# A new order for the first four tiles of a fused convolution and feed-forward kernel, and a doubling moved into an evacuation

## The chip, the cores and the metric

The kernel runs on one core of one Trainium2 chip. The metric is the time of one execution on the device in microseconds (us). Five timed runs of the kernel before gave a median of 720.44 us, from 720.09 to 720.65.

## The reference

```python
# attention part: a causal 7-tap convolution, one softmaxed filter for each of 8 heads
w = softmax(weight, axis=-1)                       # [8, 7]
x_pad = zeros of 6 rows before x                   # x is [8, 4096, 192]
out[b, s, h, g] = sum_k w[h, k] * x_pad[b, s + k, h, g]
# feed-forward part, on the 32768 rows of out
h = out @ w_in                                     # [32768, 192] @ [192, 2048]
g = h * cos(h)
result = g @ w_out                                 # [32768, 2048] @ [2048, 192]
```

Input and output are float32; the kernel computes with bfloat16 operands and float32 sums.

## The kernel before, in words

**Tiles and units.** The 32768 rows are cut into 64 tiles of 512 rows (`t`) and 32 units of 1024 rows (`u`), two tiles to a unit. For a unit the following happens. SP loads it (`load_unit`, L75, 768 KB) and the 16 rows at its block edges (`load_edges`, L69). POOL casts it to bfloat16 (`cast_unit`, L179). TensorE convolves it with banded matrices (`conv_part` through `conv_mm`, L190), in two halves of the channels called `c = 0` and `c = 1`. ACT copies each half out of PSUM into the tile `ct` (`conv_out`, L205, one copy a bank). `ct` holds each row of 64 channels twice, because the matmuls that follow run two at a time on the two halves of TensorE's rows; POOL writes the second copy (`double_unit`, L247). SP transposes `ct` into `cT` with a DMA (`turn_unit`, L253). POOL mends the first six rows of each block from the edge rows (`mend_edges`, L259).

**The feed-forward of a tile.** Eight chunks `h0` to `h7`, each six matmuls (`mm1`, L347) into one of three PSUM buffers named `h`. For each chunk ACT computes the cosine (`cs`, L354) and DVE multiplies (`g`, L358; the step is called `s0` to `s7`). The product with w_out is cut into steps (`mm2_step`, L377), 64 a tile. A step issues a matmul on the lower rows for one phase and one on the upper rows for the phase before, so that the first 32 steps of all have one matmul and the others two. The outputs gather in two PSUM banks, `o_ps0` and `o_ps1`, which ACT copies out (`evac`, L389) and SP stores (`store`, L392). Where one bank changes from the lower rows to the upper ones, and between the two parts of a split convolution, a no-operation on SP's queue (`Turn`, L164) passes the order from one matmul to the next: SP's queue carries loads, transposes, stores and these turns, in program order.

**The order is written by hand.** A string for each tile gives TensorE's order: `h3` is a chunk, `m7` seven steps, `c1` and `c2` the two parts of a conv half, `p` and `q` marks at which an output half is complete and at which DMA issues and POOL work are put. A second string gives ACT's (and with it DVE's): `s3` a cosine and a product, `ec1` and `ec2` the evacuations of a conv half, `P` and `Q` those of an output half. An entry of ACT's string is put out as soon as what it needs stands in the program. Tiles 0 and 1 have strings of their own, because there units 1 and 2 are convolved whole (the halves `d` and `c`), the other tiles use `PE_ORDER` and `ACT_ORDER`. In tile 0 a conv half uses the banks `o_ps0` and `o_ps1` (`o_banks`), from tile 1 on an `h` buffer (`ring_banks`).

**The start.** The first half of unit 0 (512 rows, which is tile 0) is convolved and transposed on TensorE (`conv_first`, `turn_first`). Its second half comes at the entry `r` in tile 0: `conv_rest`, then POOL's doubling, then the transpose by DMA, then the loads of unit 2, then POOL's two casts of w_out (L445). The loads of unit 3 and the doubling of unit 1 follow at the end of tile 0; the transpose of unit 1, the cast of unit 3 and the mending of unit 1 at `q` of tile 1.

Of the kernel before, what the change touches and what calls it, by code (L numbers as in the profile page):

```python
# [16 lines left out]
def kernel(  # L17
# [12 lines left out]
    G = D // H  # L30
# [3 lines left out]
    NB = T // 128  # L34
    U = 1024
    NU = NTOK // U
    UB = U // 128
# [149 lines left out]
    def conv_mm(u, c, ps, i, rows, n0, n1, prev=0, **flags):  # L187

        h = 4 * c + i
        return nc.tensor.matmul(  # L190
            out=ps[i // 2][:, 0 : (n1 - n0) * 2 * G].rearrange("p (n k i r) -> p i n k r", n=n1 - n0, k=NC, i=2)[:, i % 2],
            lhsT=band[rows, h, 128 if prev else 0 : 256 if prev else 128],
            rhs=bf[u][rows, n0:n1, h * G : (h + 1) * G].rearrange("p n (k r) -> p n k r", k=NC),
            skip_group_check=True, **flags)

    def conv_out(u, c, ps, n0, m0, m1, copy, double=False, banks=(0, 1)):

        for b in banks:
            w0 = (2 * c + b) * 2 * R
            o = ct_tiles[u][:, m0:m1, :, :, w0 : w0 + 2 * R].rearrange("p n k t w -> p (n k) t w")  # L200
            i = ps[b][:, (m0 - n0) * 2 * G : (m1 - n0) * 2 * G].rearrange("p (m t w) -> p m t w", t=1, w=2 * R)
            if double:
                copy(o, i.to_broadcast([128, (m1 - m0) * NC, 2, 2 * R]))
            else:
                copy(o[:, :, 0, :], i[:, :, 0, :])  # L205
# [5 lines left out]
    def o_banks():  # L211
        return [o_pools[b].tile([128, T], FP32, name="o_ps%d" % b) for b in range(2)]

    def conv_part(u, c, banks, whole=False):


        ps = banks()
        sides = [slice(0, 64), slice(64, 128)]

        def mm(i, rows, **flags):  # L220
            return conv_mm(u, c, ps, i, sides[rows], 0, UB + 1, **{"start": False, "stop": False, **flags})

        if whole:
            for i in range(4):
                conv_mm(u, c, ps, i, slice(0, 128), 0, UB + 1, start=i % 2 == 0, stop=i % 2 == 1)
            yield
        else:
            mm(0, 0, start=True)
            mm(2, 1, start=True)
            turn = Turn()  # L230
            turn.mark(mm(1, 0), mm(3, 1))
            yield
            turn.wait(mm(2, 0), mm(0, 1))
            mm(3, 0, stop=True)
            mm(1, 1, stop=True)
        yield
        if c == 0 and u not in ct_tiles:
            ct_tiles[u] = ct_pool.tile([128, UB + 1, NC, 2, 64], BF16, name="ct")
        for b in range(2):
            conv_out(u, c, ps, 0, 0, UB + 1, nc.scalar.copy, banks=(b,))  # L240
            yield
# [3 lines left out]
    def double_unit(u, n0=0, n1=UB + 1):  # L245
        ct = ct_tiles[u]
        nc.gpsimd.tensor_copy(out=ct[:, n0:n1, :, 1, :], in_=ct[:, n0:n1, :, 0, :])  # L247
# [29 lines left out]
    for i, k in enumerate("DPDPDPADPDPADPAD"):  # L277
        q, rows = divmod(i, 4)
# [5 lines left out]
    copies = [nc.scalar.copy, nc.vector.tensor_copy]  # L284
# [33 lines left out]
    def conv_rest():  # L318
        banks = o_banks()
        for c in range(2):  # L320
            for i in range(4):
                for prev in range(2):
                    conv_mm(0, c, [b[:, 4 * G * 2 * c :] for b in banks], i, slice(0, 128), NB + 1 - prev, UB + 1 - prev, prev,
                            start=c == 0 and prev == 0 and i % 2 == 0, stop=c == 1 and prev == 1 and i % 2 == 1)
        for b in range(2):
            for c in range(2):
                conv_out(0, c, [x[:, 4 * G * 2 * c :] for x in banks], NB, NB, UB, copies[1 - b], banks=(b,))

    conv_first()
    turn_first(0)  # L330
# [20 lines left out]
    def gcu(t, j, h, n0=0, n1=NB):  # L351
        cs = cos_pool.tile([128, 2, T], BF16, name="cs")
        part = slice(n0 * 128, n1 * 128)
        nc.scalar.activation(out=cs[:, :, part], in_=h[:, :, part], func=AF.Sin, bias=math.pi / 2.0, scale=1.0)  # L354
        if j == 0 and n0 == 0:
            g_tiles[t] = gpool.tile([128, NF, T], BF16, name="g")
            g_tiles.pop(t - 3, None)
        nc.vector.tensor_tensor(out=g_tiles[t][:, 2 * j : 2 * j + 2, part], in0=h[:, :, part], in1=cs[:, :, part], op=ALU.mult)  # L358
# [27 lines left out]
    def evac(t, b):  # L386
        if b == 0:
            o_sb[t] = opool.tile([128, NB, D], FP32, name="o_sb")
        nc.scalar.copy(o_sb[t][:, 2 * b : 2 * b + 2, :].rearrange("p s d -> p (s d)"), o_ps.pop((t, b))[:, 0 : 2 * D])  # L389

    def store(t, b0=0, b1=2):
# [8 lines left out]
    PE_ORDER = "h0 m7 c1 m6 c2 m4 h1 m7 q h2 h3 m12 h4 m10 h5 m10 h6 h7 p m8"  # L400
    ACT_ORDER = "s0 ec1 ec2 s1 Q s2 s3 s4 s5 P s6 s7"

    PE_FIRST = ["h0a h0b h1 r h2 h3 h4 d1 d2 h5 h6 c1 c2 h7 p m12",
                "h0 m8 h1 m12 q h2 h3 h4 m4 d1 d2 m8 h5 m8 h6 c1 c2 m8 h7 m4 p m8"]
    ACT_FIRST = ["s0a s0b s1 s2 s3 s4 ed1 ed2 s5 s6 ec1 ec2 s7", "s0 s1 s2 s3 s4 ed1 ed2 s5 s6 ec1 ec2 P s7"]

    HALVES = {"": (0, NB), "a": (0, NB // 2), "b": (NB // 2, NB)}
    step = 0
    for t in range(NT + 2):
        u, second = divmod(t, TPU)  # L410
        cu, cc = (u + TPU, second) if t >= TPU else (1 + t, 1)
        conv = {"c": conv_part(cu, cc, ring_banks if t else o_banks, t < TPU) if cu < NU else iter(())}
        if t < TPU:
            conv["d"] = conv_part(cu, 0, ring_banks if t else o_banks, True)
        act, done, h = (ACT_ORDER if t > 1 else ACT_FIRST[t]).split(), set(), {}

        def flush():
            while act:
                k = act[0]
                need = {"P": "p", "Q": "q", "e": k[1:2] + "2"}.get(k[0], "h" + k[1:])  # L420
                if need not in done:
                    return
                act.pop(0)
                if k == "P" and 0 <= t - 1 < NT:
                    evac(t - 1, 0)
                elif k == "Q" and 0 <= t - 2 < NT:
                    evac(t - 2, 1)
                elif k[0] == "e":
                    next(conv[k[1]], None)
                elif k[0] == "s" and t < NT:  # L430
                    gcu(t, int(k[1]), h.pop(k[1:]), *HALVES[k[2:]])

        for k in (PE_ORDER if t > 1 else PE_FIRST[t]).split():
            if k[0] == "h" and t < NT:
                h[k[1:]] = mm1(t, int(k[1]), *HALVES[k[2:]])
            elif k[0] in conv:
                next(conv[k[0]], None)
            elif k == "r":
                conv_rest()
                double_unit(0, NB, UB)  # L440
                turn_unit(0, NB, UB)
                load_unit(2)
                load_edges(2)
                for q in range(2):
                    nc.gpsimd.tensor_copy(out=wo[:, q * HP : (q + 1) * HP], in_=wo_f[:, q * HP : (q + 1) * HP])  # L445
            elif k[0] == "m":
                for q in range(step, step + int(k[1:])):
                    mm2_step(q)
                step += int(k[1:])
            elif k[0] == "p":  # L450
                assert step % (2 * STEPS) == 0
            elif k[0] == "q":
                assert step % (2 * STEPS) == STEPS
            done.add(k)
            flush()

            if k == "q":
                if second == 0 and t and u + 1 < NU:
                    turn_unit(u + 1)
                    mend_edges(u + 1)  # L460
                if t == 1:
                    turn_unit(1)
                    cast_unit(3)
                    mend_edges(1)
                if second == 0 and u + 3 < NU:
                    cast_unit(u + 3)
                if second == 1 and t > 1 and cu < NU:
                    double_unit(cu)
                if t == NT + 1:
                    store(NT - 1, 1, 2)  # L470
            if k == "p":
                if t < NT + 1 and 0 <= t - 2:
                    store(t - 2)
                if t == NT:
                    store(NT - 1, 0, 1)
                if second == 1 and u + 4 < NU:
                    load_unit(u + 4)
                    load_edges(u + 4)
        if t == 0:
            double_unit(1)  # L480
            load_unit(3)
            load_edges(3)
            cast_unit(2)
        if t == 1:
            double_unit(2)
# [30 lines left out]
```

## Time and profile before

| what | value |
|---|---|
| median of five timed runs | 720.44 us |
| the profiled execution, its own time | 720.38 us |
| its span | 718.7 us |
| TensorE matmul busy | 708.2 us, 99% |
| ACT busy | 617.8 us, 86% |
| DVE busy | 611.3 us, 85% |
| POOL busy | 149.8 us, 21% |
| granted TensorE clock, mean | 0.999 |

The profile is of one execution; its times count from the start of its span. "PE" is TensorE's matmuls and "PEld" its weight loads. A line such as "L377" is the line of the kernel before. In square brackets stands how long an engine was idle before an instruction, and what it waited for. Matmuls are pipelined: the length of a row of matmuls holds the depth of the last one, so that rows overlap by some 0.2 us.

### The profile page before, as it was taken

The numbers are of one execution on the slowest core, as the hardware profiler recorded it, in microseconds if no ns is written. First come the engines' busy times: TensorE is split into PE (matmuls) and PEld (weight loads), VectorE is DVE, ScalarE is ACT, GpSimd is POOL, SyncE is SP. The second block draws the span as 40 slices with busy tenths as digits, with TensorE's granted clock in tenths as the row PEclk, the third lists the DMA queues.
The fourth block names the chain that finished last, engine by engine and source line by source line (L and its number), as shares of the span: only waits on it lengthen the run. The fifth ranks groups of instructions, "written<-read, shape, count | busy, mean of one in ns | idle before, by whom it ended". The sixth has DMA issues, their size and how long they took to land.

```text
span 718.7 us, 26316 instructions
## 1 busy us (share of the span) xinstructions
PE 708.2 (99%) x11827; PEld 529.8 (74%) x11827; DVE 611.3 (85%) x536; ACT 617.8 (86%) x781; POOL 149.8 (21%) x124
## 2 busy tenths in 40 slices
PE   7899999999999999999999999999999999999997
PEld 3577777777777777777777777777777777777776
DVE  6788888888888888888888888888888888888984
ACT  7888888888888898888888888888888888888884
POOL 5621112221122221022220222220222221121000
PEclk9999999999999999999999999999999999999999
DMA  8745544455534356534455434566434555424312
GB/s 216 182 122 144 137 93 130 85 135 145 126 108 116 87 144 145 113 108 113 102 145 145 117 101 104 114 144 145 109 109 95 124 145 143 103 67 89 80 46 67
DMA packets 183664, 85.24 MB, mean 119 GB/s; under 512 B 111616, under 2 KB 183168, under 8 KB 183552
## 3 DMA queue, kind: packets, MB, share of 16 engines
q1 hardware_dynamic: 183128, 82.78, 47.0%
q8 instruction: 92, 1.51, 0.9%
q0 software_dynamic: 416, 0.79, 0.7%
q14 instruction: 20, 0.16, 0.1%
q10 hardware_dynamic: 8, 0.00, 0.0%
HBM read 31.36 MB, written 25.17 MB: 79 GB/s over the span
## 4 chain that ended last, share of the span: by engine, by line
PE 95%; DMA 2%; POOL 1%; DVE 1%; ACT 0%; issue 0%; SPq 0%; DVEq 0%; POOLq 0%
PE o_ps L377 46%; PE h L347 45%; PE h L190 3%; DMA wo_f<-in_moe_w_out_dram 1%; DMA x_f<-in_x_dram 1%; PE h L377 0%; POOL x_bf L179 0%; POOL wo L445 0%; PE o_ps L292 0%; DVE g L358 0%; DVE band L279 0%; DVEq L511 0%; ACT cs L354 0%; POOL mask L128 0%; DVE ct L298 0%
## 5 line engine op out<-in xcount | busy, mean ns | idle before, releaser
L358 DVE TENSOR_TENSOR g<-h,cs 128x1024 bf16<-128x1024 f32 (+1 forms) x513 | 603.4, 1217 | 94.0 <-ACT cs L354 89.2
L354 ACT ACTIVATE cs<-h 128x1024 bf16<-128x1024 f32 (+1 forms) x513 | 511.5, 1026 | 59.1 <-PE h L347 52.0
L377 PE MATMUL o_ps<-wo,g 64*128 64x192 bf16 x8128 | 423.8, 243 | 1.7 <-ACT o_sb L389 0.6
L377 PEld LDWEIGHTS <-g 64*128 64x128 bf16 x8192 | 362.0, 94 | 86.1 <-SPq L164 1.2
L347 PE MATMUL h<-cT,w 64*128 64x512 bf16 (+1 forms) x3078 | 398.2, 376 | 0.3 <-DVE cT L316 0.2
L347 PEld LDWEIGHTS <-w 64*128 64x128 bf16 x3078 | 154.3, 94 | 85.6 <-issue 1.1
L259 POOL COPY cT<-cT 128x144 bf16<-128x144 bf16 x31 | 9.6, 310 | 496.8 <-DMA cT<-ct 393.3
L179 POOL CAST x_bf<-x_f 128x1728 bf16<-128x1728 f32 (+1 forms) x32 | 80.6, 2518 | 8.7 <-DMA x_f<-in_x_dram 8.6
L205 ACT CAST ct<-h 128x432 bf16<-128x432 f32 x120 | 56.4, 522 | 27.4 <-PE h L190 26.9
L389 ACT COPY o_sb<-o_ps 128x384 f32<-128x384 f32 x127 | 60.0, 473 | 4.9 <-PE o_ps L377 4.9
L247 POOL COPY ct<-ct 128x1728 bf16<-128x1728 bf16 (+1 forms) x32 | 51.3, 1604 | 17.6 <-ACT ct L205 17.0
L190 PE MATMUL h<-x_bf,band 64*128 64x216 bf16 (+1 forms) x472 | 42.7, 254 | 0.9 <-POOL x_bf L179 0.9
L190 PEld LDWEIGHTS <-band 64*128 64x128 bf16 (+1 forms) x496 | 22.2, 94 | 7.1 <-issue 4.5
L105 PE MATMUL o_ps<-zero 128*128 128x512 bf16 x12 | 5.5, 630 | 1.3 <-DVE zero L100 1.3
L377 PE MATMUL h<-wo,g 64*128 64x192 bf16 x64 | 5.8, 243 | 0.0
L190 PE MATMUL o_ps<-x_bf,band 128*128 128x96 bf16 (+1 forms) x24 | 1.9, 222 | 2.5 <-POOL x_bf L179 2.5
L105 PEld LDWEIGHTS <-zero 128*128 128x128 bf16 x15 | 1.7, 129 | 3.5 <-issue 2.2
L205 ACT CAST ct<-o_ps 128x432 bf16<-128x432 f32 (+1 forms) x6 | 2.4, 460 | 1.1 <-PE o_ps L190 1.1
L445 POOL CAST wo<-wo_f 128x1536 bf16<-128x1536 f32 x2 | 2.9, 1470 | 1.0 <-DMA wo_f<-in_moe_w_out_dram 1.0
L389 ACT COPY o_sb<-h 128x384 f32<-128x384 f32 x1 | 0.5, 479 | 2.4 <-PE h L377 2.4
L115 ACT ACT_TABLE_LOAD x1 | 1.3, 1283 | 1.4 <-PEq L500 1.4
L292 PEld LDWEIGHTS <-band 128*128 128x128 bf16 x32 | 1.1, 102 | 1.1 <-POOL band L279 1.0
(47 smaller groups left out, 27.7 us busy)
## 6 DMA issues: line engine op xcount, KB each, us to landing
out_dram<-o_sb SPq DMA_DIRECT2D x63, 384.0 KB
x_f<-in_x_dram SPq DMA_DIRECT2D x31, 768.0 KB
x_f<-in_x_dram SPq DMA_DIRECT2D x31, 96.0 KB
wo_f<-in_moe_w_out_dram SPq DMA_DIRECT2D x4, 384.0 KB
x_f<-in_x_dram SPq DMA_DIRECT2D x2, 384.0 KB
w<-in_moe_w_in_dram POOLq DMA_DIRECT2D x2, 384.0 KB, 6.2
cT<-ct SPq DMA_TRANSPOSE x32
out_dram<-o_sb SPq DMA_DIRECT2D x2, 192.0 KB
```

Of the source, the lines that this page charges most:

```text
L105: nc.tensor.matmul(out=bank, lhsT=zero[:, 0:128], rhs=zero, start=True, stop=True)
L179: copy(out=bf[u][:, n0 + o : n1 + o, :].rearrange("p n (h k r) -> p (n h) k r", k=NC, r=R), in_=x_tiles[u][:, n0:n1, :].rearrange("p n (h ...
L190: return nc.tensor.matmul(out=ps[i // 2][:, 0 : (n1 - n0) * 2 * G].rearrange("p (n k i r) -> p i n k r", n=n1 - n0, k=NC, i=2)[:, i % 2], ...
L205: copy(o[:, :, 0, :], i[:, :, 0, :])
L247: nc.gpsimd.tensor_copy(out=ct[:, n0:n1, :, 1, :], in_=ct[:, n0:n1, :, 0, :])
L259: nc.gpsimd.tensor_copy(out=cT[u][:, 0:UB, :, 0 : K - 1], in_=cT[u][:, UB].rearrange("p c (n t) -> p n c t", t=16)[:, :, :, 8 : 8 + K - 1])
L347: nc.tensor.matmul(out=h[:, i, n0 * 128 : n1 * 128], lhsT=w[rows, k, j, :], rhs=c[rows, m0 + n0 : m0 + n1, k, :], start=(k == 0), stop=(k ...
L354: nc.scalar.activation(out=cs[:, :, part], in_=h[:, :, part], func=AF.Sin, bias=math.pi / 2.0, scale=1.0)
L358: nc.vector.tensor_tensor(out=g_tiles[t][:, 2 * j : 2 * j + 2, part], in0=h[:, :, part], in1=cs[:, :, part], op=ALU.mult)
L377: m = nc.tensor.matmul(out=o_ps[tt, b][:, si * D : (si + 1) * D], lhsT=g_tiles[tt][rows, f, s * 128 : (s + 1) * 128], rhs=wo[rows, f // 2, ...
L389: nc.scalar.copy(o_sb[t][:, 2 * b : 2 * b + 2, :].rearrange("p s d -> p (s d)"), o_ps.pop((t, b))[:, 0 : 2 * D])
L445: nc.gpsimd.tensor_copy(out=wo[:, q * HP : (q + 1) * HP], in_=wo_f[:, q * HP : (q + 1) * HP])
```

## The change

The doubling of the second half of unit 0 is no longer a POOL copy after the evacuation; the evacuation itself writes both copies, on DVE and ACT, as `conv_first` does. The transpose of that half then follows `conv_rest` directly, still behind the four loads of w_out and ahead of the loads of unit 2 in SP's queue. Tiles 0 to 3 get new strings. In tile 0, `h2` stands before `r` and `h5` before the conv halves, and the 12 steps at its end go to tile 1; tile 1 begins with 8 steps and ends with `h7`; tiles 2 and 3 have strings of their own, of which tile 2's begins with 9 steps, the first conv part and 1 step before `h0`. At the end of tile 3 as many steps have been put out as before (200), and from tile 4 on the strings are the same. The number of instructions differs on POOL alone, which has one less.

```diff
         for b in range(2):
             for c in range(2):
-                conv_out(0, c, [x[:, 4 * G * 2 * c :] for x in banks], NB, NB, UB, copies[1 - b], banks=(b,))
+                conv_out(0, c, [x[:, 4 * G * 2 * c :] for x in banks], NB, NB, UB, copies[1 - b], True, (b,))
...
-    PE_FIRST = ["h0a h0b h1 r h2 h3 h4 d1 d2 h5 h6 c1 c2 h7 p m12",
-                "h0 m8 h1 m12 q h2 h3 h4 m4 d1 d2 m8 h5 m8 h6 c1 c2 m8 h7 m4 p m8"]
-    ACT_FIRST = ["s0a s0b s1 s2 s3 s4 ed1 ed2 s5 s6 ec1 ec2 s7", "s0 s1 s2 s3 s4 ed1 ed2 s5 s6 ec1 ec2 P s7"]
+    PE_FIRST = ["h0a h0b h1 h2 r h3 h4 h5 d1 d2 h6 h7 c1 c2 p",
+                "m8 h0 m2 h1 m11 h2 m7 h3 m4 q h4 m9 d1 d2 m7 h5 m7 h6 m1 c1 c2 m8 p h7",
+                "m9 c1 m1 h0 m6 c2 m9 h1 m7 q h2 h3 m15 h4 m5 h5 m12 p h6 h7",
+                "m8 c1 m6 c2 m5 h0 m9 h1 m3 h2 m1 q h3 m14 h4 m7 h5 m11 h6 h7 p m8"]
+    ACT_FIRST = ["s0a s0b s1 s2 s3 s4 s5 ed1 ed2 s6 ec1 ec2 s7", "s0 s1 s2 s3 s4 ed1 ed2 s5 s6 P ec1 ec2 s7",
+                 "s0 ec1 ec2 s1 Q s2 s3 s4 s5 P s6 s7", "ec1 ec2 s0 s1 Q s2 s3 s4 s5 P s6 s7"]
...
             elif k == "r":
                 conv_rest()
-                double_unit(0, NB, UB)
                 turn_unit(0, NB, UB)
```

More of the change, by code (lines that the diff above doesn't have):

```diff
@@ L414 @@
             conv["d"] = conv_part(cu, 0, ring_banks if t else o_banks, True)
-        act, done, h = (ACT_ORDER if t > 1 else ACT_FIRST[t]).split(), set(), {}
+        act, done, h = (ACT_ORDER if t >= len(ACT_FIRST) else ACT_FIRST[t]).split(), set(), {}
         def flush():
@@ L431, in flush @@
                     gcu(t, int(k[1]), h.pop(k[1:]), *HALVES[k[2:]])
-        for k in (PE_ORDER if t > 1 else PE_FIRST[t]).split():
+        for k in (PE_ORDER if t >= len(PE_FIRST) else PE_FIRST[t]).split():
             if k[0] == "h" and t < NT:
```

## The prediction

> **What bounds the kernel now.** First the page: TensorE is busy 99% of the span, and the chain that ended last is 95% TensorE. So the time is TensorE's work plus the time in which TensorE waits, and a new order of the same instructions can only change the waits.
>
> ```profile
> span 718.7 us, 26316 instructions
> PE 708.2 (99%) x11827; PEld 529.8 (74%) x11827; DVE 611.3 (85%) x536; ACT 617.8 (86%) x781; POOL 149.8 (21%) x124
> PEclk9999999999999999999999999999999999999999
> PE 95%; DMA 2%; POOL 1%; DVE 1%; ACT 0%; issue 0%; SPq 0%; DVEq 0%; POOLq 0%
> ```
>
> Second, stretches of 5 us (columns: stretch, length, then busy time of PE, PEld, DVE, ACT, POOL, granted clock, DMA share, GB/s). From 35 us on TensorE is never free until the tail at 706; all that a new start can win lies before.
>
> ```profile
> 10.00:15.00 5.00, 3.75 (x49) 2.18 (x48) 3.90 (x7) 3.31 (x8) 1.35 (x2) 1.00 1.10 323
> 15.00:20.00 5.00, 3.59 (x32) 1.58 (x30) 3.67 (x4) 4.81 (x7) 4.57 (x3) 1.00 0.88 249
> 20.00:25.00 5.00, 4.43 (x50) 3.30 (x48) 4.32 (x4) 4.16 (x6) 3.04 (x2) 1.00 1.01 251
> 25.00:30.00 5.00, 3.98 (x52) 2.49 (x50) 4.51 (x5) 3.85 (x6) 3.61 (x2) 1.00 1.19 271
> 35.00:40.00 5.00, 5.00 (x93) 3.98 (x90) 2.63 (x3) 3.89 (x6) 0.65 (x1) 1.00 0.62 182
> ```
>
> Third, the timeline of TensorE (start, length, what, count, idle time before). Five named waits, 4.6 us: unit 0's second half (L190, 13.14), unit 1's cast (17.44), the evacuation that frees the o banks (21.17), unit 2's cast (28.75), the evacuation of tile 0's output (34.82).
>
> ```profile
> 13.14 0.84 PE L190 MATMUL o_ps<-x_bf,band 128*128 128x96 bf16 x16 [1.07 <-POOL x_bf L179]
> 17.44 0.53 PE L190 MATMUL o_ps<-x_bf,band 128*128 128x216 bf16 x4 [1.41 <-POOL x_bf L179]
> 21.17 1.08 PE L377 MATMUL o_ps<-wo,g 64*128 64x192 bf16 x11 [0.57 <-ACT ct L205]
> 28.75 0.53 PE L190 MATMUL h<-x_bf,band 128*128 128x216 bf16 x4 [0.93 <-POOL x_bf L179]
> 34.82 0.84 PE L377 MATMUL o_ps<-wo,g 64*128 64x192 bf16 x16 [0.59 <-ACT o_sb L389]
> ```
>
> Fourth, POOL and SP, which set when those casts can run.
>
> ```profile
> 17.33 0.83 POOL L247 COPY ct<-ct 128x768 bf16<-128x768 bf16 x1
> 26.16 2.53 POOL L179 CAST x_bf<-x_f 128x1728 bf16<-128x1728 f32 x1 [2.52 <-DMA x_f<-in_x_dram]
> 33.35 0.31 POOL L259 COPY cT<-cT 128x144 bf16<-128x144 bf16 x1 [1.89 <-DMA cT<-ct]
> 18.18 1.54 SPq L253 DMA_TRANSPOSE cT<-ct  x1
> 19.78 0.90 SPq L75 DMA_DIRECT2D x_f<-in_x_dram  x1
> 25.45 4.68 SPq L253 DMA_TRANSPOSE cT<-ct  x1
> ```
>
> Unit 0's doubling (17.33) waits behind POOL's cast of unit 1, SP's transpose behind the doubling, unit 2's load behind the transpose, and unit 2's cast and conv (28.75) behind the load.
>
> **The base.** At 34.82 the kernel before has all 16 h chunks, 64 w_out steps and units 1 and 2 convolved. The kernel after has the same at the end of tile 1. From there to the end of tile 3 both do 136 steps, 16 h and 4 split convs, and from tile 4 on the orders are equal. So the gain is 34.82 less the time at which the new tile 1 ends, less new waits in tiles 2 and 3.
>
> Units of TensorE, from the chain in order of time: an h chunk 0.65, a step 0.0825 (16 matmuls, 8 steps, 0.66; in the first 32 steps one matmul a step, at nearly that pace), a whole conv half 0.46 (17.44 to 17.90), unit 0's rest 0.77 (13.14 to 13.91), a split conv 0.19. An h chunk's result reaches ACT 0.87 after its start. Queued back to back, cosine copies follow every 0.92 and products every 1.13. h has three buffers, so each chunk or ring conv needs the third one before it released.
>
> **Tile 0.** h2 now stands ahead of unit 0's rest. It needs g0a, done at 12.45, so it runs 12.50 to 13.15 in the wait that ended at 13.14: 0.65 won. Rest to 13.92, h3 to 14.57, h4 to 15.22. The second product of that stretch, g2, runs 14.42 to 15.64.
>
> The doubled evacuation: four copies that write 384 elements instead of 192, two on DVE and two on ACT. Shown: 0.35 (DVE) and 0.32 (ACT) for 192; 0.56 and 0.48 for 384 without the repeated read (L316); 0.96 and 0.80 for 768 with it (L298). I take 0.56 and 0.48, as the size is the same: +0.42 on DVE, +0.32 on ACT; the upper end, 768's price each, adds 0.8 more on DVE; below nothing is excluded, since they write more. It delays g3, and with it g4 and h7, so it is on the path of tile 0. It removes POOL's 0.83 at 17.33: POOL's w_out cast starts 17.35 instead of 18.10, which nothing waited for.
>
> DVE: copies to 16.56, g3 16.48 to 17.70, g4 to 18.83, g5 to 19.96. h5 at 15.70 (after g2). Then TensorE waits for unit 1's cast as before, to 17.44: first conv half, h6 at 17.90, h7 at 18.88 (after g4), second half 19.53 to 20.0, its first evacuation 19.91 to 20.43.
>
> **Tile 1.** The 12 steps that stood at 21.17 are gone from tile 0; m8 starts at 20.50, behind that evacuation. Then h0 21.16, m2, h1 21.98, m11, h2 23.54, m7, h3 24.77, m4 to 25.75, h4 to 26.40, m9 to 27.14, with no wait that I can find: w_out's second cast (20.61 to 22.08) is wanted at 23.1, g7 (done 23.04) at 23.54. h0 needs unit 0's transposed second half. It landed at 22.01, 3.8 after its issue; issued after DVE's copies at 16.62 instead of 18.18, and queued behind w_out, whose packets thin out at 18.3, I put it at 20.9. Unmoved, it would cost 0.85 at h0.
>
> The first conv half then needs unit 2's cast. Its load is issued 1.56 earlier (18.22); cast before began 6.38 after issue. The bare shift gives 24.60 and a cast end at 27.14: no wait. But the queue was 88% to 110% busy from 10 us on. The row shows a near-idle piece only around 19 us, so the shift is between nothing (conv at 28.75) and 1.56 (27.14); I take 1.15, conv at 27.55, because that idle piece, about 1 us, is what can be filled.
>
> After the conv starts: two halves 0.92, 23 steps 1.90, three chunks 1.95, and 0.11 for h7 waiting on g5: 4.88. Tile 1 ends at 32.43. The last wait of before (34.82) has h7 as cover now: ACT's evacuation is done at about 32.4. **34.82 - 32.43 = 2.39 won.**
>
> At this place the Trainium skill's page "DMA: Bandwidth & Descriptors", section "Anatomy of one DMA", fits a DMA of the software path as about 2 us plus bytes over 436 GB/s, an estimate of 3.8 us for unit 2's 768 KB. The trace has 5.5 from issue to landing. By the page the cast would never be late, and the win would be 2.80. I go by the row.
>
> **Tiles 2 and 3.** m9, c1 and m1 now stand before h0, which therefore starts at 33.45 instead of directly. It needs unit 1's transpose and the mend of its edges (POOL). That transpose is queued behind the step at q, 26.05 instead of 25.45. All 31 long transposes took 6.05 to 7.93 from issue to the start of the mend (0.31); so the mend ends at 32.4 to 34.3, and h0 waits 0 to 0.85. I take 0.3 (about half of them took under 7). SP issues for 4.1 to 4.7 in it, and the next thing SP must pass on, the bank turn of step 63, comes at 31.9, behind it. In tile 2 the unit 2 transpose issues 37.2 to 41.4, and the turn of step 127 is due at 42.4: 1 us spare. In tile 3 h3 waits about 0.15 for g0, and the Q evacuation ends as m14 wants its bank. Sum: 0.45 lost.
>
> **Net 2.39 - 0.45 = 1.94.** The profiled execution took 720.38 (span 718.7 and 1.7 around it), 0.06 under the median of 720.44. 720.38 - 1.94 = 718.44, and I say 718.4.
>
> On the clock: the rows grant 1.00 in every stretch from 0 to 130, through waits of up to 1.41; the longest new wait is 1.09 (16.35 to 17.44), so I book nothing. The page "TensorE: Matmul & The Clock Gate", Part 1, halves the clock after an idle window of about 3.4 us. By it a dropped window would cost about 1.7 as an estimate, but no gap here comes near.
>
> **Rivals.**
> 1. Unit 2's load is not earlier: the queue is full whatever SP does, or the transpose is issued no sooner. For it: DMA share of about 1 from 20 to 30. Against: the thin piece at 18.5 to 19.5. Conv at 28.75, tile 1 ends 33.63, won 1.19, less 0.3 to 0.45: 719.5. Not told from no change, which here means within 0.2%, 1.44 us.
> 2. Slower: unit 1's transpose takes the place of the casts. It is issued 0.6 later, h0 of tile 2 is wanted 2.0 sooner (33.45 for 35.47), and everything on TensorE is queued behind h0. Each us past 33.45 costs one. The gain, less the 0.15 in tile 3, is used up when the mend ends at 35.7, with a transpose of 9.3, and slower begins at 37.1, with 10.8; the worst row is 7.93. With 12 (an estimate, half as long again as the worst) the mend ends at 38.36: 4.9 + 0.15 - 2.39 = 2.7 lost, 723.0. Against it: unit 2 and 3's loads, which ran into the transpose before, are out of the way sooner.
> 3. The best case: the full shift and no wait for the mend: 2.80 - 0.15, 717.7.
>
> **Numbers.** Forecast (717.9 to 719.0) 0.58; best case 0.14; load unmoved 0.21; slower 0.04; 0.03 for something not seen. Range 717.4 to 719.8: it takes in the best case and the unmoved load. Faster by over 0.2% (under 719.0) 0.73, within 0.21, slower 0.06.
>
> **What would show it.** Right: h2 before 13.1 with no wait at the rest; SP's first transpose near 16.6; unit 2's cast near 25.0 and its conv near 27.6; TensorE without a wait from 20.5 to there; tile 2 begun near 32.4; mend over by 34. Wrong: the conv still at 28.7; a wait at tile 2's first h chunk over 1 us; a wait at tile 1's h0; waits on SP's turns; a granted clock under 1 before 35.

## The result, and the profile after

The kernel after takes 718.76 us (median of 23 runs, 718.41 to 719.41), the kernel before 720.51 in the runs beside it (41 runs). The ratio is 0.9976, with a 95% interval of 0.997 to 0.9982: 1.75 us faster, where 1.94 was forecast (718.4, range 717.4 to 719.8). The profiled execution took 718.85, its span is 717.1.

The page after (span, engines, clock and the chain that ended last): the same picture, 1.6 us shorter. POOL has one instruction less; the total is one higher (26317 for 26316), because there are two more semaphore instructions, which the engines' counts leave out.

```profile
span 717.1 us, 26317 instructions
...
PE 707.7 (99%) x11827; PEld 529.8 (74%) x11827; DVE 611.7 (85%) x536; ACT 618.3 (86%) x781; POOL 149.0 (21%) x123
...
PEclk9999999999999999999999999999999999999999
...
PE 96%; DMA 2%; POOL 1%; DVE 0%; ACT 0%; DVEq 0%; issue 0%; SPq 0%; POOLq 0%
```

The stretches of 5 us after (columns as before: PE, PEld, DVE, ACT, POOL, clock, DMA share, GB/s). From 25 us on TensorE is busy without a break, 10 us sooner than before; from 20 to 25 it is less busy than before (4.07 for 4.43).

```profile
10.00:15.00 5.00, 4.41 (x55) 2.43 (x54) 3.97 (x6) 4.21 (x9) 1.26 (x2) 1.00 1.10 325
15.00:20.00 5.00, 3.74 (x32) 1.52 (x26) 5.00 (x7) 4.85 (x7) 3.89 (x2) 1.00 1.28 250
20.00:25.00 5.00, 4.07 (x42) 2.65 (x41) 3.51 (x4) 3.81 (x5) 3.04 (x2) 1.00 1.01 272
25.00:30.00 5.00, 5.00 (x74) 3.69 (x74) 4.79 (x5) 4.05 (x6) 4.35 (x2) 1.00 0.94 165
```

The timeline of TensorE after (up to about L400 a line has the same number as in the kernel before). Unit 0's rest (13.24), the conv of unit 2 (28.01) and the steps of tile 2 (33.02) have no wait any more, and h2 fills most of the wait that stood ahead of the rest. A new wait of 0.51 stands at tile 1's first chunk (21.93), on the transposed second half of unit 0.

```profile
12.48 0.82 PE L347 MATMUL h<-cT,w 64*128 64x512 bf16 x6 [0.41 <-DVE g L358]
13.24 0.85 PE L190 MATMUL o_ps<-x_bf,band 128*128 128x96 bf16 x16
...
17.53 0.53 PE L190 MATMUL o_ps<-x_bf,band 128*128 128x216 bf16 x4 [1.02 <-POOL x_bf L179]
...
20.59 0.83 PE L377 MATMUL o_ps<-wo,g 64*128 64x192 bf16 x8 [0.43 <-ACT ct L205]
...
21.93 0.82 PE L347 MATMUL h<-cT,w 64*128 64x512 bf16 x6 [0.51 <-DMA cT<-ct]
...
28.01 0.53 PE L190 MATMUL h<-x_bf,band 128*128 128x216 bf16 x4
...
33.02 0.92 PE L377 MATMUL o_ps<-wo,g 64*128 64x192 bf16 x18
```

The chain of waits after, in order of time (start, length): the transpose of unit 0 carries it for 5.25 us, from its issue at 16.64 to the first chunk of tile 1.

```profile
14.95 1.69 POOL x_bf L179
16.64 5.25 DMA cT<-ct
21.89 0.05 issue
21.93 0.82 PE h L347 x6
```

POOL and SP after. Unit 2's cast begins at 25.40 (26.16 before), the mend is over at 33.63 (33.66 before). SP's transpose starts 1.54 sooner but occupies SP for 2.65 instead of 1.54, so unit 2's load is issued only 0.39 sooner.

```profile
25.40 2.56 POOL L179 CAST x_bf<-x_f 128x1728 bf16<-128x1728 f32 x1 [1.74 <-DMA x_f<-in_x_dram]
...
33.32 0.31 POOL L259 COPY cT<-cT 128x144 bf16<-128x144 bf16 x1 [2.56 <-DMA cT<-ct]
...
16.64 2.65 SPq L253 DMA_TRANSPOSE cT<-ct  x1
...
19.39 0.52 SPq L75 DMA_DIRECT2D x_f<-in_x_dram  x1
...
26.85 4.86 SPq L253 DMA_TRANSPOSE cT<-ct  x1
```

### The profile page after: what moved, and what is told of

It reads as the page before. It is cut to its first block, busy times and chain, and to the rows that moved or that the text cites. A ratio compares the mean times of both kernels' runs of the same rounds, so it can differ in the third digit from the quotient of the medians.

```text
span 717.1 us, 26317 instructions
## 1 busy us (share of the span) xinstructions
PE 707.7 (99%) x11827; PEld 529.8 (74%) x11827; DVE 611.7 (85%) x536; ACT 618.3 (86%) x781; POOL 149.0 (21%) x123
## 4 chain that ended last, share of the span: by engine, by line
PE 96%; DMA 2%; POOL 1%; DVE 0%; ACT 0%; DVEq 0%; issue 0%; SPq 0%; POOLq 0%
PE o_ps L377 47%; PE h L347 45%; PE h L190 3%; DMA x_f<-in_x_dram 1%; DMA cT<-ct 1%; PE h L377 0%; POOL x_bf L179 0%; DVE g L358 0%; DVEq L513 0%; ACT cs L354 0%; POOL mask L128 0%; SPq L75 0%; ACT mask L133 0%; DVE diag L269 0%; DVE prod L266 0%
## 5 line engine op out<-in xcount | busy, mean ns | idle before, releaser
L247 POOL COPY ct<-ct 128x1728 bf16<-128x1728 bf16 x31 | 50.5, 1628 | 18.2 <-ACT ct L205 18.0
```

## The experiments

A transfer "lands" when the last of its parts does; the trace records 16 for each load of w_out and for each transpose. Two theories stood at the start. Theory W: unit 0's transpose cannot finish before the last packets of w_out ahead of it, so an earlier issue gains nothing. Theory I: it takes a set time from its own issue. "Won" below is against the kernel before in the same batch (720.51 to 720.63); the change itself won 1.75. The intervals of the ratios reach about 0.1% (0.7 us) to each side, so smaller differences are read from the profiles, each of one execution, and not from the times.

**1. The new orders with POOL's doubling.**

```diff
-copies[1 - b], True, (b,))
+copies[1 - b], banks=(b,))
                 conv_rest()
+                double_unit(0, NB, UB)
```

> The new orders with the doubling of unit 0's second half back on POOL. DVE and ACT each save two times 0.2, but SP's transpose waits for POOL's copy (17.4 to 18.25) and issues near 18.3 instead of 16.64. Theory W (the transpose cannot finish before the last packets of w_out, which land at 20.5 in both kernels): it lands near 22.0 as in the kernel before and after, and the first chunk of tile 1 starts near 22.0; only the load of unit 2 is later (issue near 19.9), its conv at 28.7 instead of 28.0, so about 0.7 is lost: 719.5. Theory I (the transpose follows its own issue, 5.25 later as in the kernel after): it lands near 23.5, the first chunk of tile 1 is 1.6 late, about 1.6 lost: 720.4.

Measured: 719.81, ratio 0.9991 (0.9982 to 1.0), 0.81 won. The chain of waits of this kernel:

```profile
17.67 0.82 POOL ct L247
...
18.52 3.82 DMA cT<-ct
22.35 0.05 issue
22.39 0.84 PE h L347 x6
```

The transpose was issued 1.88 later than in the kernel after and landed 0.46 later. Theory I wanted 23.5; W fits, with a floor of 3.82 from issue to landing. The conv of unit 2 came at 29.13. Two things held it within 0.1: its cast, over at 29.08, and its PSUM buffer, because the products behind the late chunk ran later.

```profile
29.13 0.53 PE L190 MATMUL h<-x_bf,band 128*128 128x216 bf16 x4 [0.60 <-DVE g L358]
...
26.54 2.54 POOL L179 CAST x_bf<-x_f 128x1728 bf16<-128x1728 f32 x1 [3.00 <-DMA x_f<-in_x_dram]
```

So on top of the new orders the doubled evacuation is worth about half of the win: 0.94 by the gains, 0.99 by the two profiled executions (719.84 and 718.85).

**2. The doubling alone, in the old orders.**

> The orders of before with the doubling in the evacuation alone. The transpose issues near 15.4 instead of 18.18, the load of unit 2 about 1 earlier. Theory W: the transpose still lands near 22, so the first chunk of tile 1 stays near 22.0; the conv of unit 2 moves from 28.75 to 27.8 to 28.2, 0.4 to 0.9 won: 719.6 to 720.1. Theory I: the transpose lands near 20.7, which the steps ahead of that chunk hide, and the win is the same 0.9 at most. The doubled copies cost DVE 0.42 and should cost the end nothing, since TensorE waits for unit 1's cast behind them.

Measured: 720.21, ratio 0.9994 (0.9985 to 1.0003), 0.41 won, not clear of none by its interval. Issued 2.7 sooner than in the kernel before, the transpose landed at 22.46, later than the 22.01 there. It occupied SP for 4.22:

```profile
15.49 4.22 SPq L253 DMA_TRANSPOSE cT<-ct  x1
...
19.82 0.52 SPq L75 DMA_DIRECT2D x_f<-in_x_dram  x1
...
25.92 2.54 POOL L179 CAST x_bf<-x_f 128x1728 bf16<-128x1728 f32 x1 [1.70 <-DMA x_f<-in_x_dram]
```

Theory I (20.7) falls. But the conv of unit 2, which I expected at 27.8 to 28.2, came at 28.65, only 0.10 sooner than before. It waited for its PSUM buffer; its cast was over at 28.46.

```profile
28.65 0.55 PE L190 MATMUL h<-x_bf,band 128*128 128x216 bf16 x4 [0.49 <-DVE g L358]
```

In this execution unit 1's cast also began 0.27 later than in the kernel before (15.14 for 14.87), and with it everything behind. It took 720.39, as long as the one of before (720.38), so no gain is shown for the doubling alone. The two parts of the change, 0.41 and 0.81, give 1.22 one by one and 1.75 together; that difference is within the intervals.

**3. The transpose ahead of the fourth load of w_out.**

```diff
-    def load_wo(q):
-        for i in range(2):
+    def load_wo(q, i0=0, i1=2):
+        for i in range(i0, i1):
...
         load_wo(0)
-        load_wo(1)
+        load_wo(1, 0, 1)
...
                 turn_unit(0, NB, UB)
+                load_wo(1, 1, 2)
```

> The kernel after, with the transpose of unit 0's second half ahead of the fourth load of w_out in SP's queue. Theory W: with three loads of w_out ahead of it, which land at 18.3, the transpose lands near 20 to 21 and the first chunk of tile 1 starts at 21.25 without a wait (0.7 earlier). Theory I: it still lands near 21.9, as it is issued at the same 16.6. By both, the load of unit 2 is no earlier than in the kernel after (the fourth load now lies between), so its conv stays near 28.0 to 28.4 and the time near 718.8 to 719.2: the wait only moves from the chunk to the conv.

Measured: 719.61, ratio 0.9986 (0.9977 to 0.9994), 1.01 won. The transpose, issued at 16.69, landed at 20.68, and the wait at tile 1's first chunk is gone: W again. But the fourth load of w_out now landed at 22.67, its cast came 2.1 later, and the steps and the conv waited for the casts (w_out's cast has line L448 in this kernel):

```profile
24.25 0.40 PE L377 MATMUL o_ps<-wo,g 64*128 64x192 bf16 x3 [0.81 <-POOL wo L448]
...
28.77 0.53 PE L190 MATMUL h<-x_bf,band 128*128 128x216 bf16 x4 [0.36 <-POOL x_bf L179]
```

I had expected 718.8 to 719.2, the time of the kernel after. That w_out's second cast had only 1 us to spare stood in the prediction (done at 22.08, wanted at 23.1), and I did not take it into account.

**4. Without the transpose.**

```diff
-                turn_unit(0, NB, UB)
+                ct_tiles.pop(0)
...
+    nc.gpsimd.memset(cT[0][:, NB:UB].rearrange("p n c k -> p (n c k)"), 0.0)
```

> The kernel after without the transpose of unit 0's second half; that half of the transposed tile is filled with zeros instead, so that the outputs of 512 rows are left out. It prices all that the transpose costs. No wait at the first chunk of tile 1 (21.25 instead of 21.93), and the load of unit 2 right behind w_out, so that its conv follows TensorE at 27.2 to 27.3 without a wait: 0.7 won, tile 2 at 32.3 instead of 33.02. Whether tile 2's first chunk (then 33.3) has to wait for the mend depends on unit 1's transpose: issue 26.1 plus 6.05 to 7.93 gives a mend end of 32.4 to 34.3, so 0 to 1.0 of it may go there: 718.0 to 718.8.

Measured: 718.15, ratio 0.9965 (0.9953 to 0.9978), 2.47 won. TensorE has no wait over 0.12 between 20.66 and the tail; tile 2 begins at 32.41 instead of 33.02. The transpose thus costs the kernel after 0.6 to 0.7. More went than the transfer itself: SP no longer waits for the evacuation either, so unit 2's load is issued at 13.65 instead of 19.39, and its cast begins at 23.50.

**5. The old strings for tiles 2 and 3** (tile 2's with `m8` in front).

> The kernel after with the old strings for tiles 2 and 3; tile 2's begins with eight steps more (m8 ahead of h0), as the new tile 1 ends at step 64. In the kernel after no new wait shows in tile 2, and 0.17 in tile 3 (a chunk that waits for the product of the first). If the new strings of tiles 2 and 3 only cost that wait, it is 0.2 faster: 718.6. If they cover the mend of unit 1's edges (over at 33.63, and h0 would stand at 33.68 instead of 34.03), it is 0 to 0.7 slower, depending on that transpose: up to 719.4.

Measured: 718.48, ratio 0.9972 (0.9962 to 0.9983), 2.03 won. No wait shows in tiles 2 and 3. The transpose of unit 0 also landed 0.15 sooner in this execution; that and the missing wait of 0.18 are the 0.34 by which the two profiled executions differ (718.51 and 718.85). The mend was over at 33.11 and wanted at 33.52. The new strings of tiles 2 and 3 bring nothing here.

**6. More steps ahead of tile 1's first chunk.**

```diff
-"m8 h0 m2 h1 m11 h2 m7 h3 m4 q h4 m9 d1 d2 m7 h5 m7 h6 m1 c1 c2 m8 p h7"
+"m16 h0 h1 m5 h2 m11 q h3 m5 h4 m11 d1 d2 m2 h5 m5 h6 m1 c1 c2 m8 p h7"
-"m8 c1 m6 c2 m5 h0 m9 h1 m3 h2 ...
+"m8 c1 m6 c2 m3 h0 m9 h1 m5 h2 ...
```

> The kernel after with tile 1 in another order: 16 steps ahead of its first chunk, which then stands at 21.93 where the transpose lands, and steps moved ahead of the conv of unit 2; in tile 3 two steps move behind the first chunk, so that its product is ready earlier. No wait of over 0.2 at tile 1's first chunk (0.51 now) or at tile 3's h3 (0.17). Worked out as in the prediction, tile 1 ends at 32.5 instead of 33.02 and tile 3 loses nothing: 0.6 won, 718.1. If the transpose of unit 0 were not what holds tile 1, nothing would be won: 718.6 to 718.8.

Measured: 718.24, ratio 0.9971 (0.996 to 0.9982), 2.27 won. TensorE's timeline of this kernel: 16 steps bridge the time to the landing (21.46 in this execution, 0.43 sooner than in the kernel after's), tile 2 starts at 32.34 instead of 33.02, and in tile 3 h3 (48.26) follows its step directly.

```profile
20.54 1.33 PE L377 MATMUL o_ps<-wo,g 64*128 64x192 bf16 x14 [0.43 <-ACT ct L205]
21.63 0.39 PE L347 MATMUL h<-cT,w 64*128 64x512 bf16 x1
...
32.34 0.92 PE L377 MATMUL o_ps<-wo,g 64*128 64x192 bf16 x18
...
48.16 0.26 PE L377 MATMUL o_ps<-wo,g 64*128 64x192 bf16 x2
48.26 0.82 PE L347 MATMUL h<-cT,w 64*128 64x512 bf16 x6
```

In the kernel after the last pair stands 0.18 further apart than the step takes:

```profile
48.72 0.26 PE L377 MATMUL o_ps<-wo,g 64*128 64x192 bf16 x2
48.98 0.82 PE L347 MATMUL h<-cT,w 64*128 64x512 bf16 x6
```

**7. Unit 0's rest ahead of h2 again** (`"h0a h0b h1 r h2 h3 h4 h5 ..."`).

> The kernel after with unit 0's rest back ahead of h2 in tile 0. The wait of about 1.0 at the rest comes back, and h2 and its product run about 0.7 later. By the prediction's step (0.65 won there) the time is 0.65 longer: 719.4. By the theory that tile 0 is covered twice, by the cast of unit 1 (the conv cannot start before 17.4 to 17.8) and by the transpose that lands at 21.9 whatever tile 0 does, at most 0.1 to 0.3 is lost: 718.9 to 719.1; the last steps of tile 0 are then 0.5 later and the wait at tile 1's first chunk shrinks by that.

Measured: 718.79, ratio 0.9977 (0.9968 to 0.9986), 1.72 won, as the kernel after. Its profiled execution took 720.32, 1.5 over its median, so only its start is read: tile 1's steps begin at 21.29 instead of 20.59, and its first chunk follows them with no wait in the profile, 0.05 after the transpose landed (22.11).

```profile
21.29 0.83 PE L377 MATMUL o_ps<-wo,g 64*128 64x192 bf16 x8 [0.55 <-ACT ct L205]
22.16 0.82 PE L347 MATMUL h<-cT,w 64*128 64x512 bf16 x6
```

So of the 0.70 by which this tile 0 is later, 0.23 is left at the chunk: what h2 wins in tile 0, the wait for the transpose takes back.

**8. The fourth load of w_out from POOL's queue.**

> The kernel after with the fourth load of w_out issued from POOL instead of SP, so that the transpose of unit 0's second half stands behind three loads in SP's queue. If it is the place in the queue that holds the transpose, it lands near 20.6 as with the fourth load behind it (20.7 there, 21.9 in the kernel after), w_out is complete by 20, the first chunk of tile 1 starts at 21.3 without a wait, and the load of unit 2 is no later than now: the conv stays bound by the cast, 27.3 to 28.0, 0 to 0.7 won: 718.1 to 718.8. If it is the amount of w_out still on the engines, the transpose lands at 21.9 as now and the time is 718.8.

Measured: 718.60, ratio 0.9974 (0.9963 to 0.9984), 1.91 won, the kernel after within noise. The transpose landed at 21.80 and the wait is still there:

```profile
21.85 0.82 PE L347 MATMUL h<-cT,w 64*128 64x512 bf16 x6 [0.54 <-DMA cT<-ct]
```

So it is not the number of loads ahead in SP's queue. The third load was now the last one ahead; its last of 16 parts landed at 20.47, the other 15 by 18.26. The fourth, from POOL's queue, landed at 20.35 to 20.63.

**9 and 10. On top of 6: tile 0's second conv half in an `h` buffer behind 16 steps; and the old strings for tiles 2 and 3.**

> The kernel with more steps first, with tile 0's second conv half of unit 1 in an h buffer instead of the o banks and the 16 steps ahead of it, so that they wait only for the first half's evacuation (18.4) and w_out's first cast (18.9): TensorE goes on at 19.5 instead of waiting 0.43 for the second half's evacuation at 20.5. TensorE is then ready for tile 1's first chunk near 21.4, and the transpose of unit 0 (landing 21.4 to 21.9) and the cast of unit 2 (end 27.5 to 28) bind. If they leave room, up to 0.4 is won: 717.8 to 718.0; if not, nothing: 718.2 to 718.3.

> The kernel with more steps first, with the old strings for tiles 2 and 3 (m8 ahead of tile 2's first chunk). That kernel has no wait over 0.15 in its own tiles 2 and 3, so the old strings can only be as fast, 718.2 to 718.3, or lose where the first chunk of tile 2, 0.34 earlier, meets the mend of unit 1 (over at 32.5 to 33.6 by the transpose's 6.05 to 7.9, wanted at 33.0): up to 718.9.

Measured: 718.17 (ratio 0.9967, 0.9955 to 0.998) and 718.13 (0.9966, 0.9954 to 0.9978). Both beat the kernel before by 2.5 and the kernel after by its median, and neither can be told from 6 by its time. In 9 TensorE is ready sooner and waits 0.43 at tile 1's first chunk until the transpose lands (21.80): the transpose is the floor.

## Why the prediction was right

The base held. The whole difference lies before tile 4: from there the transposes of the two kernels stand 1.63 apart (61.15 and 59.52), and all but two later ones stay so to the end.

**Tile 0** went by the working: h2 at 12.48 (12.50 forecast), the copies 0.55 on DVE and 0.47 to 0.50 on ACT (0.56 and 0.48), tile 1's steps at 20.59 (20.50). The doubled copies cost no more than the row of the same size said. But the 0.65 counted as won at h2 is no part of the win: run 7 takes it back, and its median is only 0.03 longer, far within the noise.

**The step that was mis-sized** is "I put it at 20.9": the landing of unit 0's transpose. It came at 21.89, near the "unmoved" case, and cost 0.77 at h0 (21.93 for 21.16), of the 0.85 that the text priced. A wait at tile 1's h0 was one of the prediction's own signs of being wrong. The 20.9 was a guess between 20.4 (3.8 after the issue) and 22.01. What the profiles show in its place, in all eleven kernels with the transpose: it lands 1.31 to 1.34 after the last part of the load ahead of it, or 3.83 after its own issue, whichever is later.

| run | issue | last part ahead landed | transpose landed |
|---|---|---|---|
| before | 18.18 | 20.55 | 22.01 |
| 1, POOL doubles | 18.52 | 20.44 | 22.35 |
| after | 16.64 | 20.56 | 21.89 |
| 2, doubling alone | 15.49 | 21.12 | 22.46 |
| 3, ahead of the fourth load | 16.69 | 19.35 | 20.68 |
| 5, old strings | 16.61 | 20.40 | 21.74 |
| 6, more steps | 16.59 | 20.15 | 21.46 |
| 7, rest ahead of h2 | 15.47 | 20.77 | 22.11 |
| 8, fourth load from POOL | 16.53 | 20.47 | 21.80 |
| 9, conv in the ring | 16.59 | 20.47 | 21.80 |
| 10, 6 with old strings | 16.60 | 20.75 | 22.09 |

The first two rows sit on 3.83, the others on the bound by the load (run 3 shows both within 0.2). The trace's packet records show how. In the kernel after, the transpose has 1536 packets of 256 bytes (run 4 has none of that size there); 508 of them start by 19.26, then none until 0.05 after w_out's last packet of 768 bytes has started (19.98), and the rest run from 20.03 to 21.37. In the other early-issued ones (runs 2, 5 to 10) the same stop comes after 502 to 507, ends 0.04 to 0.13 after w_out's last packet on SP's queue, and the rest takes 1.34 to 1.35. That last part is not late because of the transpose: in run 4, which has none, it landed at 20.46 too. The hint was in the profile before: I saw that packets "thin out at 18.3" and took this for the end of w_out, though POOL's cast of its last part waited to 20.61. The bytes moved before, from 16 to 23 us in slices of 0.175 us, and that cast:

```profile
GB/s 316 338 320 320 342 329 312 334 397 307 320 307 268 206 114 40 9 9 9 34 178 231 224 149 35 253 290 279 249 186 226 160 158 48 39 35 127 303 334 347
...
20.61 1.47 POOL L445 CAST wo<-wo_f 128x1536 bf16<-128x1536 f32 x1 [1.03 <-DMA wo_f<-in_moe_w_out_dram]
```

**Unit 2's load** was the other half of that: 1.15 was taken for the shift of its cast, 0.76 came, as SP was held 2.65 by the transpose and issued the load at 19.39 instead of 18.22. The cast ended at 27.96, and TensorE, 0.8 late from h0, got to the conv at 28.01 (27.55 forecast). By these rows either of the two alone would have put the conv at 28.0. (The text reads the DMA share as 88% to 110% from 10 us on; the rows from 25 to 35 give 1.19 and 0.31. The forecast does not rest on them.)

**The rest**: from the conv to tile 2, 4.88 forecast and 5.01 measured. **Tiles 2 and 3**: 0.3 was booked for the mend and none came (over at 33.63, wanted at 34.03). Unit 1's transpose was issued at 26.85, 0.8 later than forecast, but took only 6.46 to the mend, out of a range of 6.05 to 7.93. That was luck of this execution: with 6.46 the forecast times would have given no wait either, and with 7.93 from 26.85 the mend would have come 1.06 too late. For h3 in tile 3 0.15 was booked, 0.18 measured. Sum: 1.80 won at tile 2 for 2.39, 0.18 lost for 0.45, 1.63 from 60 us on for 1.94 (the whole profiled executions differ by 1.53, the medians by 1.75). Two errors, of 0.59 and 0.27, partly cancelled; that the forecast came so near is in part luck.

**The rivals.** Unit 2's load did move, so the unmoved case fell. The slow case fell by its price: unit 1's transpose took 6.46 to the mend, not 9.3. The clock stayed at 1.00 in every stretch, through waits of up to 1.02 in the kernel after and 1.69 in run 2; no run here had an idle window as long as the one in the Trainium skill's "TensorE: Matmul & The Clock Gate", Part 1. Unit 2's load took 5.1 from issue to landing (19.39 to 24.45). The estimate of 3.8 from the skill's "DMA: Bandwidth & Descriptors", section "Anatomy of one DMA", which the page gives for the software path, is short of that for this load from SP's queue, as it was for the kernel before (5.5); the measurement decides.

## What to carry to other kernels

When one engine is at 99%, only its waits can be won, and a win at one wait is kept only up to the next thing that lands at a set time; walk each resource forward to that floor before adding savings up. An earlier issue is not an earlier landing: ask what stands ahead in the queue and when its last part, not its bulk, lands. Where a landing can't be moved, put work that doesn't need it ahead of the instruction that does (runs 6, 9 and 10: 2.27 to 2.50 won), which won as much, within the noise, as taking the transfer out (run 4: 2.47).

## What the runs showed of the hardware

The transpose and the load ahead of it hold each other up. The moved bytes of the kernel after from 16 to 23 us (40 slices of 0.175 us, in GB/s) fall to 18 to 22 for over 1 us while the transpose stands still after a third of its packets and w_out is not complete; all 16 parts of w_out's last load then land together, at 20.46 to 20.56. ("DMA" is the busy share of the engines in tenths.)

```profile
DMA  9999999999999999999000000999999989999999
GB/s 329 338 316 325 329 334 401 307 298 329 312 290 298 287 258 199 124 97 38 22 22 22 18 19 18 257 291 288 295 285 340 281 219 334 355 351 347 351 342 338
```

In the kernel before, 15 of the 16 landed by 19.35 and one at 20.55. In all twelve profiles a 16 KB packet of the instruction queue starts at 16.9 to 17.6 and runs for 1.1 to 1.2 us, and the late part lags by much the same: 1.20 in the kernel before, 1.17 in the third load of the kernel after (0.81 in run 1 and 0.71 in run 4). The records do not name the engine, and no run moved that packet, so that it is what holds the part back is not shown.

For the long transposes the time goes with the same packets (a pattern in two profiles, not a trial). Of the 62 in the two profiles, 20 had no such packet between 0.4 after issue and the mend; they took 6.05 to 6.62, 16 of them 6.05 to 6.08; in three of the four others one had started just before, at 0.39 to 0.40. Of the 42 with one, all but one (whose packet came at the very end) took 6.20 to 7.93, and every one over 7.5 had its packet 5.0 to 5.7 after issue, at the transpose's last packets.

Issuing unit 0's transpose occupies SP for 1.54 behind an emptying queue (before and run 1), 2.26 to 2.74 when issued at 16.5 to 16.7, and 4.22 in run 2, issued at 15.49. In run 7, issued at 15.47, it took 2.57; why these two differ is open.
